# Second MLP layer of the last 12 token tiles by Strassen's algorithm, with combined weights in buffers of attention

## The chip, the core and the metric

The kernel runs on one core of a Trainium2 chip. The core has five engines that run side by side, each in its own order: TensorE (PE) multiplies matrices into PSUM, VectorE (DVE), ScalarE (ACT) and GpSimd (POOL) work element by element, and SyncE (SP) issues transfers. They meet only at semaphores. The metric is the device time of one execution in microseconds, lower is better; the median of several runs is given.

## What is computed

Cosine attention over 8 batches, 12 heads, 448 positions and head size 64, then a mixer: a low-rank mix over positions and a two-layer MLP of 768 to 3072 to 768.

```python
q_n, k_n = q / norm(q), k / norm(k)
attn = softmax(q_n @ k_n.T / tau) @ v          # (8, 12, 448, 64)
x = attn.transpose(0, 2, 1, 3).reshape(8, 448, 768)
u = x + ((x.transpose(0, 2, 1) @ U) @ V).transpose(0, 2, 1)
out = u + np.maximum(u @ w_ch1, 0.0) @ w_ch2   # (8, 448, 768), float32
```

## The kernel before

Two batches of 448 tokens make seven token tiles of 128, so there are 28 tiles in four pairs of batches. The MLP works in units: a batch of even number takes three tiles, one of odd number four. In the first layer of a unit (`up`, L942) a block of 128 hidden features is made for all tokens of the unit at once: six matmuls of 384 or 512 columns accumulate in one PSUM bank, and ScalarE or VectorE moves it through relu (L965, L967) into the one `relu` buffer, which holds 24 such blocks. In the second layer (L978) each tile's two halves of 384 output columns are 24 matmuls each, whose stationary operand is a 128 x 128 block of relu and whose moving operand is a row block of `w2_t`. VectorE adds u (L989), and SP stores the result in rows (L1003). All matmul operands are bf16, the sums and the output are float32.

Before its MLP a unit needs u, with tokens in the partitions, and its transpose `uT`, with features in the partitions. From the third batch on SP makes it by transposing DMAs (L900) into the one `uT` buffer.

Attention of later batches runs between the MLP matmuls: scores (L686) in bursts of three slots, exponentials on ScalarE (L704), products with v (L731), a reciprocal and a multiplication on VectorE (L760, L762), the low-rank projection (L815) and u (L865, L879). Queries and keys are squared, summed and scaled on VectorE and ScalarE before (L549, L553, L557, L625). Loads are issued by GpSimd's queue (L501, L524, L529), and they end some 200 us before the end.

Nothing is timed at run time. The program writes down every operation with an estimated duration, its dependences, the buffers that it takes and gives back (`Slot`, `Ring`) and a priority; `Plan.run` lays them out engine by engine, and the instructions are issued in that order. The order of streams on TensorE is fixed in a list, with the MLP's stream last, so that attention goes first where it is ready. Score bursts of batch b + 2 are tied to points of the MLP of batch b by the table `SPOTS`.

```python
work = [(i, t, c0, c0 + CH) for i, t in enumerate(tiles) for c0 in (0, CH)]
if b == B - 1:
    i, t, c0, c1 = work.pop()
    mid = c1 - 96
    work += [(i, t, c0, mid), (i, t, mid, c1)]
```

The last half tile of all is thus split into 288 and 96 columns, so that the last addition and its stores are small.

Names that the change touches: `ld_t`, `xn_t` (loaded and scaled queries and keys), `r_sq` (squares), `v_t` (v of two batches), `r_uT`, `r_relu`, `r_O` (three output tiles), `stage0` (projection and u), `mlp`, and the list of units at the end of the program.

Of the kernel before, what the change touches and what calls it, by code (L numbers as in the profile page):

```python
# [11 lines left out]
FP = mybir.dt.float32  # L12
BF = mybir.dt.bfloat16
# [256 lines left out]
def kernel(  # L270
# [42 lines left out]
    def fixed(n, shape, dt, name):  # L313

        tiles = [const.tile(shape, dt, name=f"{name}{i}") for i in range(n)]
        return tiles

    def ring(n, shape, dt, name, space=None):
        p = space or pool
        return Ring(n, lambda i: p.tile(shape, dt, name=name, tag=name, bufs=n))  # L320

    def fixed_ring(tiles):
        return Ring(len(tiles), lambda i: tiles[i % len(tiles)])

    ld_t = fixed(3, [SCH, 2, G, SC * D], BF, "qk_nat")
    xn_t = fixed(3, [SCH, 2 * SC, 128], BF, "xn")
# [5 lines left out]
    r_sq = ring(3, [SCH, G // 2, SC * D], BF, "sq")  # L332
# [8 lines left out]
    r_uT = ring(1, [128, CC, 512], BF, "uT")  # L341

    w2_t = const.tile([128, NC, C], BF, name="w2_sb")
    r_relu = Ring(1, lambda i: pool.tile([128, 4 * R + S + 4 * SC * D], FP, name="raw_uv", tag="relu", bufs=1)
                  if i == 0 else pool.tile([128, NC, 512], BF, name="relu", tag="relu", bufs=1))
# [17 lines left out]
    r_O = ring(3, [128, CH], FP, "O_sb")  # L363
# [129 lines left out]
    got, last_exp = {}, {}  # L493
# [278 lines left out]
    prev, first_v = {}, {}  # L772
# [3 lines left out]
    def columns(X, A, uT, muls, cc, a):  # L776

        c0 = 128 * cc
        mm = Slot(r_z, 1)
        st = pe_z[cc]  # L780
        X.uses += 1
        X.left += 1
        A.uses += 1
        A.left += 1
        for t in range(3):
            plan.add(Op("PE", 0.055, lambda t=t: nc.tensor.matmul(  # L786
                out=mm.tile[:, 128 * t:128 * (t + 1)], lhsT=X.tile[:, t, c0:c0 + 128], rhs=ident,
                start=(t == 0), stop=False, skip_group_check=True),
                deps=muls[2 * cc:2 * cc + 2] + [id_set] if t == 0 else (), acq=[mm, uT] if t == 0 else [],
                rel=[X] if t == 2 else []), st)  # L790
        o = plan.add(Op("PE", pe_t(384), lambda: nc.tensor.matmul(
            out=mm.tile[:, 0:384], lhsT=A.tile[:, c0:c0 + 128], rhs=V_sb[:, PAD:PAD + 384],
            start=False, stop=True, skip_group_check=True), deps=[a], rel=[A]), st)
        cs = []
        mm.uses = mm.left = 1 if cc < CC - 1 else 2
        for n in range(mm.uses):
            e, r = ("ACT/DVE", slice(0, 384)) if cc < CC - 1 else (("ACT", "DVE")[n], slice(192 * n, 192 * n + 192))
            c = plan.add(Op(e, any_t(384 // mm.uses), None, deps=[o], rel=[mm], prio=0 if cc < CC - 1 else -1))
            c.fn = lambda c=c, r=r: copy_op(c, uT.tile[:, cc, r], mm.tile[:, r])
            cs.append(c)  # L800
        return cs

    def stage0(b, X, muls):
# [6 lines left out]
        uT = Slot(r_uT, NC * CC)  # L810
# [77 lines left out]
        if by_pe:  # L888
            for ccs in ((0, 1), (2, 3), (4,), (5,)):
                z = max(0, ccs[0] - 3)  # L890
                ins = [(lambda u=u, cc=cc: u.tile[:, cc * 128:(cc + 1) * 128])
                       for cc in ccs for u in us]
# [4 lines left out]
                               [adds[z, i] for i in range(len(tiles))], [uT], list(us)))  # L897
        else:
            for i, u in enumerate(us):
                ut.append(plan.add(Op("SP", 0.1, lambda i=i, u=u: nc.sync.dma_start_transpose(  # L900
                    out=uT.tile[:, :, i * 128:(i + 1) * 128], in_=u.tile),
                    deps=[adds[0, i], adds[1, i]], acq=[uT], rel=[u], prio=0,
                    lat=("x", 0.05 * 48, 2.0))))
# [17 lines left out]
    def mlp(b, us, uT, ut):  # L921
        par = b % 2
        tiles = range(3) if par == 0 else range(3, 7)
# [3 lines left out]
        if b == B - 1:  # L927
            i, t, c0, c1 = work.pop()
            mid = c1 - 96
            work += [(i, t, c0, mid), (i, t, mid, c1)]  # L930
            us[i].uses += 1
            us[i].left += 1
# [7 lines left out]
        def up(f, mm, ccs):  # L940
            for cc in ccs:
# [5 lines left out]
                    acq=[mm] if cc == 0 else [], rel=[uT]), pe_mlp)  # L947
# [24 lines left out]
        for group in groups:  # L972
# [12 lines left out]
            for (i, t, c0, c1), mm in zip(group, mms):  # L985
# [6 lines left out]
                for bb in (b - par, b - par + 1):  # L992
                    o0 = (bb % 2) * S
                    lo, hi = max(128 * t, o0), min(128 * (t + 1), o0 + S)
                    if lo >= hi:
                        continue
                    for nn, j, p0, p1 in segments(lo - o0, hi - o0):
                        r0 = nn + o0 - 128 * t
                        by = "ACT" if 96 < w < CH and p1 - p0 < SCH else "SP"
                        O.uses += 1  # L1000
                        O.left += 1
                        plan.add(Op(by, 0.1, lambda bb=bb, j=j, p0=p0, p1=p1, r0=r0, O=O, c0=c0, c1=c1, by=by:
                            (nc.scalar if by == "ACT" else nc.sync).dma_start(  # L1003
                                out=rows(out[bb], j, p0, p1)[:, c0:c1],
                                in_=O.tile[r0:r0 + p1 - p0, 0:c1 - c0]),
                            deps=[o], rel=[O], prio=2, lat=("x", (p1 - p0) * w * 4 / 200e3, 2.0)))

        todo = bursts.get(b + 2, ()) if b else ()
# [151 lines left out]
    for b in range(B):  # L1160
        mlp(b, *state[b])
# [46 lines left out]
```

## Time and profile before

| what | value |
| --- | --- |
| runs | 578.81, 580.06 and 578.80 us, median 578.81 |
| profiled execution, first to last instruction | 576.6 us |
| TensorE clock granted, mean | 0.999 |
| L978, second layer, 128 x 384 | x1320, mean 326 ns |
| L942, first layer, 128 x 512 | x557, mean 379 ns |
| L942, first layer, 128 x 384 | x576, mean 326 ns |
| L965, relu on ACT, 128 x 512 | x84, mean 597 ns |
| L989, output addition on DVE, 128 x 384 | x55, mean 555 ns |
| L900, transposes of u by SP | x21, 3.2 us to landing |
| L1003, stores of 144 and 48 KB by SP | 2.2 and 1.8 us to landing |
| L1003, last stores, 42 and 6 KB by SP | 1.6 and 1.5 us to landing |

How to read it: a line stands for one place in the program, with the shape of its output, how often it ran and the mean duration. Matmuls overlap in TensorE's pipeline, so the mean of one is longer than the distance from one to the next. Some matmul records are missing (557 of 576). A row of slices divides the span into 40 equal parts and gives the busy share in tenths. The profiled execution is one; its span leaves out what lies before the first and after the last instruction, so it is 2.2 us below the median of the runs.

### The profile page before, as it was taken

The numbers are of one execution on the slowest core, as the hardware profiler recorded it, in microseconds if no ns is written. First come the engines' busy times: TensorE is split into PE (matmuls) and PEld (weight loads), VectorE is DVE, ScalarE is ACT, GpSimd is POOL, SyncE is SP. The second block draws the span as 40 slices with busy tenths as digits, with TensorE's granted clock in tenths as the row PEclk, the third lists the DMA queues.
The fourth block names the chain that finished last, engine by engine and source line by source line (L and its number), as shares of the span: only waits on it lengthen the run. The fifth ranks groups of instructions, "written<-read, shape, count | busy, mean of one in ns | idle before, by whom it ended". The sixth has DMA issues, their size and how long they took to land.

```text
span 576.6 us, 11689 instructions
## 1 busy us (share of the span) xinstructions
PE 567.7 (98%) x4851; PEld 326.9 (57%) x4871; DVE 286.7 (50%) x683; ACT 286.9 (50%) x475; POOL 100.3 (17%) x144
## 2 busy tenths in 40 slices
PE   8999999999999999999999999999999999999997
PEld 6565556444655665555456655564456666654565
DVE  7989969985775877386226820253012340100011
ACT  7967655577516763584645445534445344024300
POOL 8526141240050122005000400000000000000000
PEclk9999999999999999999999999999999999999999
DMA  9999998895597839567457924440040100310021
GB/s 156 205 206 141 210 194 126 126 127 78 100 101 138 108 35 144 107 109 52 57 89 119 113 14 69 95 72 2 0 69 28 43 14 15 83 41 1 2 54 56
DMA packets 132821, 50.46 MB, mean 88 GB/s; under 512 B 97920, under 2 KB 132768, under 8 KB 132768
## 3 DMA queue, kind: packets, MB, share of 16 engines
q0 software_dynamic: 72352, 25.73, 39.4%
q1 hardware_dynamic: 60384, 23.97, 20.9%
q8 instruction: 38, 0.62, 0.5%
q14 instruction: 15, 0.12, 0.1%
q10 hardware_dynamic: 32, 0.02, 0.0%
HBM read 52.02 MB, written 11.01 MB: 109 GB/s over the span
## 4 chain that ended last, share of the span: by engine, by line
PE 94%; DVE 3%; ACT 1%; issue 1%; DMA 0%; DVEq 0%
PE bank L978 39%; PE bank L942 38%; PE bank L731 8%; PE bank L686 6%; PE bank L865 2%; DVE xn L625 1%; DVE ss L557 1%; ACT attn L699 1%; PE bank L815 1%; PE bank L479 1%; DMA raw_uv<-in_q_dram 0%; DVE X_sb L762 0%; ACT sq L549 0%; DVE qkT L1019 0%; PE bank L786 0%
## 5 line engine op out<-in xcount | busy, mean ns | idle before, releaser
L978 PE MATMUL bank<-w_sb,relu 128*128 128x384 bf16 (+2 forms) x1368 | 233.4, 323 | 0.0
L942 PE MATMUL bank<-uT,w_sb 128*128 128x384 bf16 (+1 forms) x1133 | 228.3, 352 | 1.3 <-issue 0.5
L704 ACT ACTIVATE attn<-bank 128x896 bf16<-128x896 f32 (+1 forms) x163 | 139.0, 917 | 88.6 <-PE bank L686 88.4
L978 PEld LDWEIGHTS <-relu 128*128 128x128 bf16 x1368 | 127.1, 98 | 90.7 <-issue 13.6
L942 PEld LDWEIGHTS <-w_sb 128*128 128x128 bf16 x1152 | 109.4, 98 | 103.2 <-issue 7.0
L965 ACT ACTIVATE relu<-bank 128x512 bf16<-128x512 f32 (+1 forms) x159 | 86.8, 547 | 122.6 <-PE bank L942 122.2
L989 DVE TENSOR_TENSOR O_sb<-bank,u_nat 128x384 f32<-128x384 f32 (+2 forms) x57 | 31.2, 548 | 204.0 <-PE bank L978 178.8
L557 DVE TENSOR_REDUCE ss<-sq 112x8 f32<-112x512 bf16 x96 | 62.2, 673 | 6.9 <-ACT sq L549 6.4
L731 PEld LDWEIGHTS <-attn 128*128 128x128 bf16 (+1 forms) x1536 | 54.7, 97 | 10.9 <-issue 3.5
L625 DVE TENSOR_TENSOR xn<-qk_nat,inv 112x512 bf16<-112x512 bf16 x93 | 60.6, 681 | 0.1
L731 PE MATMUL bank<-v_nat,attn 128*128 128x65 bf16 (+1 forms) x1536 | 57.5, 193 | 0.9 <-DVE X_sb L762 0.4
L686 PE MATMUL bank<-qkT 64*128 64x448 bf16 (+1 forms) x384 | 46.9, 355 | 1.2 <-ACT qkT L1017 0.5
L501 POOL DMA_DIRECT2D qk_nat<-in_q_dram x24 | 17.5, 727 | 149.4 <-ACT attn L704 37.2
L524 POOL DMA_DIRECT2D v_nat<-in_v_dram x42 | 31.1, 745 | 67.7 <-PE bank L731 52.4
L762 DVE TENSOR_TENSOR X_sb<-bank,rd 128x256 bf16<-128x256 f32 x96 | 39.1, 417 | 1.6 <-DVE rd L760 0.2
L549 ACT ACTIVATE sq<-qk_nat 112x512 bf16<-112x512 bf16 x55 | 32.3, 630 | 8.3 <-DVE ss L557 8.3
L760 DVE RECIPROCAL rd<-bank 128x4 f32<-128x4 f32 x96 | 16.7, 177 | 30.3 <-PE bank L731 29.7
L879 DVE TENSOR_TENSOR u_nat<-bank,X_sb 128x384 bf16<-128x384 f32 (+2 forms) x45 | 22.0, 527 | 9.7 <-PE bank L865 9.3
L686 PEld LDWEIGHTS <-qkT 64*128 64x128 bf16 (+1 forms) x384 | 13.0, 96 | 23.5 <-issue 17.7
L967 DVE TENSOR_SCALAR relu<-bank 128x384 bf16<-128x384 f32 (+1 forms) x33 | 19.8, 601 | 11.6 <-PE bank L942 11.1
L529 POOL DMA_DIRECT2D v_nat<-in_v_dram x28 | 17.4, 626 | 8.8 <-DMA w_sb<-in_moe_w_ch_dram 5.0
L501 POOL DMA_DIRECT2D qk_nat<-in_k_dram x24 | 16.8, 702 | 3.7 <-DMA w_sb<-in_moe_w_ch_dram 3.7
(64 smaller groups left out, 189.0 us busy)
## 6 DMA issues: line engine op xcount, KB each, us to landing
qk_nat<-in_q_dram POOLq DMA_DIRECT2D x23, 224.0 KB, 4.8
qk_nat<-in_k_dram POOLq DMA_DIRECT2D x23, 224.0 KB, 5.8
w_sb<-in_moe_w_ch_dram POOLq DMA_DIRECT2D x4, 1152.0 KB, 17.7
w_sb<-in_moe_w_ch_dram POOLq DMA_DIRECT2D x8, 576.0 KB, 16.5
out_dram<-O_sb SPq DMA_DIRECT2D x15, 168.0 KB, 2.5
out_dram<-O_sb SPq DMA_DIRECT2D x16, 144.0 KB, 2.2
out_dram<-O_sb SPq DMA_DIRECT2D x16, 120.0 KB, 2.0
v_nat<-in_v_dram POOLq DMA_DIRECT2D x11, 168.0 KB, 7.5
```

The costliest lines, as they stand in the source:

```text
L501: ops = [load(lambda i=i, src=src: nc.gpsimd.dma_start(out=ld.tile[:, i, lo:lo + h1 - h0, :], in_=src[b, h0:h1].rearrange("h (s c) d -> s ...
L549: nc.scalar.activation(out=y, in_=x, func=AF.Square)
L557: lambda i=i, a0=a0, a1=a1, sq=sq: nc.vector.reduce_sum(ss.tile[:, i, a0:a1, :].rearrange("p h c -> p (h c)"), sq.tile[:, 0:a1 - a0, :].re ...
L625: nc.vector.tensor_mul(dst, src, sc)
L686: nc.tensor.matmul(out=out, lhsT=qkT.tile.rearrange("p b s -> p (b s)")[r, n0:n0 + w], rhs=qkT.tile[r, SC:2 * SC, :].rearrange("p c s -> p ...
L704: exps.append(plan.add(Op("ACT", act_t(2 * S, 0.08), lambda sc=sc, c=c, attn=attn: nc.scalar.activation(out=attn.tile[:, :, off:off + S] i ...
L731: nc.tensor.matmul(out=av.tile[:, t, 0:D + 1], lhsT=tail.tile[:, hh, 128 * t:128 * (t + 1)] if tail and j == SC - 1 else (attn if j < SC - ...
L762: muls.append(plan.add(Op("DVE", dve_t(256), lambda av=av, rd=rd, h=h: nc.vector.tensor_mul(X.tile[:, :, h * D:(h + 1) * D], av.tile[:, :, ...
L942: o = plan.add(Op("PE", pe_t(n), lambda cc=cc: nc.tensor.matmul(out=mm.tile[:, 0:n], lhsT=w1_sb[:, cc, f * 128:(f + 1) * 128], rhs=uT.tile ...
L965: nc.scalar.activation(out=relu.tile[:, f, 0:n], in_=mm.tile[:, 0:n], func=AF.Relu)
L978: nc.tensor.matmul(out=mm.tile[:, 0:c1 - c0], lhsT=relu.tile[:, f, i * 128:(i + 1) * 128], rhs=w2_t[:, f, c0:c1], start=(f == 0), stop=(f ...
L989: nc.vector.tensor_add(out=O.tile[:, 0:w], in0=mm.tile[:, 0:w], in1=us[i].tile[:, c0:c1]),
```

## The change

The first 16 tiles keep the plain second layer, in units of 3, 4, 3, 3 and 3 tiles (`UNITS`; units now cross the borders of batches). The last 12 tiles are done in six pairs. For a pair, relu is seen as 2 x 2 blocks: two tiles of tokens by even and odd blocks of hidden features; `w2_t` as even and odd row blocks by two column halves. In Winograd's form of Strassen's algorithm the product of 2 x 2 blocks takes seven block products, each of 12 matmuls with 384 columns, in place of eight.

- The first layer of a pair has 256 columns for each matmul; two hidden blocks, even and odd, share one bank and one relu of 512.
- Sums of relu blocks (S1, S2, S4, and one that overwrites a block that is no longer needed) are made on VectorE, 16 additions of 128 x 384 a pair.
- Combinations of weight blocks are made once on VectorE, 16 subtractions of 128 x 1152: T1 and T2 go into the space of the loaded and scaled queries and keys (now one tensor, `qk_t`), T4 into that of v and of the squares, and one overwrites a quarter of `w2_t`, after the last plain unit.
- Products share banks where their sums allow it. p1 is copied out by ScalarE, GpSimd adds u to it three times, and VectorE adds the banks of the other products to the results, partly while the bank goes on accumulating the next one.
- Intermediate results use seven output tiles: the three of before, and four in the unused ends of `uT` and `relu`. Those and several other buffers become fixed tensors.
- The score bursts of the last batch are tied to points of the first two pairs. The split of the last half tile goes; the store code moves to `store`.

In the counts of instructions, TensorE has 768 + 504 second-layer matmuls of 384 columns where it had 1320 and 24 each of 288 and 96; in the first layer 576 of 384, 144 of 512 and 864 of 256, where it had 576 of 384 and 576 of 512. GpSimd has 18 additions where it had none, ScalarE six more copies.

```diff
-    ld_t = fixed(3, [SCH, 2, G, SC * D], BF, "qk_nat")
-    xn_t = fixed(3, [SCH, 2 * SC, 128], BF, "xn")
+    qk_t = const.tile([128, 3 * QC + 3 * 2 * SC * 128], BF, name="qk_all")
+    ld_t = [qk_t[0:SCH, QC * i:QC * (i + 1)].rearrange("p (i h x) -> p i h x", i=2, h=G) for i in range(3)]
...
+    spare = [uT_t[:, CC * 256:].bitcast(FP), relu_t[:, 84 * 128:].bitcast(FP)]
+    r_O2 = fixed_ring([x[:, CH * i:CH * (i + 1)] for x in spare for i in range(2)] + O_t)
...
+    def seven_weights(after, qk_free, v_free):
...
+        for j0 in range(0, HF, 3):
+            x = slice(j0, j0 + 3)
+            a = minus(T1[:, x], B_[:, x, 0, 1], B_[:, x, 0, 0], qk_free)
+            c = minus(T2[:, x], B_[:, x, 1, 1], T1[:, x], [a])
+            d = minus(t4(j0), B_[:, x, 1, 0], T2[:, x], [c, *v_free])
+            e = minus(B_[:, x, 0, 1], B_[:, x, 1, 1], B_[:, x, 0, 1], [a, *after])
...
+    def mlp_seven(tiles, right, made_by):
...
+        for j in range(HF):
+            mm = Slot(r_up, 1)
+            for e in range(2):
+                for cc in range(CC):
+                    o = plan.add(Op("PE", pe_t(256), lambda j=j, e=e, cc=cc, mm=mm: nc.tensor.matmul(
+                        out=mm.tile[:, 256 * e:256 * e + 256], lhsT=w1_sb[:, cc, (2 * j + e) * 128:(2 * j + e + 1) * 128],
+                        rhs=uT.tile[:, cc, :], start=(cc == 0), stop=(cc == CC - 1)),
...
+                a = sums(lambda x=x: nc.vector.tensor_add(S1[:, x], Q[:, x, 1], Q[:, x, 3]),
+                         [ready[i][1] for i in range(j - 2, j + 1)])
+                c = sums(lambda x=x: nc.vector.tensor_sub(S2[:, x], S1[:, x], Q[:, x, 0]), [a])
+                d = sums(lambda x=x: nc.vector.tensor_sub(S4[:, x], Q[:, x, 2], S2[:, x]), [c])
+                e_ = sums(lambda x=x: nc.vector.tensor_sub(Q[:, x, 1], Q[:, x, 0], Q[:, x, 1]), [a])
...
+        p1 = product(1, a, True, False)
+        cp = plan.add(Op("ACT", 0.42, lambda: nc.scalar.copy(out=s1.tile, in_=a.tile[:, 0:CH]),
+                         deps=[p1], acq=[s1], prio=-0.5))
+        y = [plan.add(Op("POOL", 1.0, lambda y_=y_, u=u, c0=c0: nc.gpsimd.tensor_add(
+            out=y_.tile, in0=s1.tile, in1=u.tile[:, c0:c0 + CH]), deps=[cp], acq=[y_], rel=[s1, u]), pool_q)
+            for y_, u, c0 in ((y12, u1, CH), (y22, u2, CH), (y21, u2, 0))]
+        p6 = product(6, b, True, False)
+        z12 = dve(bank(tile_of(y12), tile_of(y12), b), [p6, y[0]])
+        p2 = product(2, a, False, True, [cp])
+        x11 = dve(bank(tile_of(o11), lambda: u1.tile[:, 0:CH], a), [p2], [o11], [a, u1])
+        store(tiles[0], 0, CH, o11, x11)
+        p7 = product(7, b, False, False, [z12])
+        z22 = dve(bank(tile_of(y22), tile_of(y22), b), [p7, y[1]])
+        p5 = product(5, c, True, False)
+        x22 = dve(bank(tile_of(y22), tile_of(y22), c), [p5, z22])
+        store(tiles[1], CH, C, y22, x22)
+        p4 = product(4, b, False, True, [z22])
+        x21 = dve(bank(tile_of(y21), tile_of(y21), b), [p4, y[2]], (), [b])
+        store(tiles[1], 0, CH, y21, x21)
+        p3 = product(3, c, False, True, [x22])
+        x12 = dve(bank(tile_of(y12), tile_of(y12), c), [p3, z12], (), [c])
+        store(tiles[0], CH, C, y12, x12)
...
-        if b == B - 1:
-            i, t, c0, c1 = work.pop()
-            mid = c1 - 96
-            work += [(i, t, c0, mid), (i, t, mid, c1)]
...
-    for b in range(B):
-        mlp(b, *state[b])
+    UNITS = [[(0, 0), (0, 1), (0, 2)], [(0, 3), (0, 4), (0, 5), (0, 6)], [(1, 0), (1, 1), (1, 2)],
+             [(1, 3), (1, 4), (1, 5)], [(1, 6), (2, 0), (2, 1)]]
+    for b, tiles in enumerate(UNITS):
+        mlp(b, tiles, *(state[b] if b < PE_BATCHES else columns_of(tiles)))
+    rest = [(z, t) for z in range(2, 4) for t in range(7)][2:]
...
+    for n in range(0, len(rest), 2):
+        hosts.append(mlp_seven(rest[n:n + 2], *seven))
+    (t0, l0), (t1, l1) = hosts[:2]
+    for o, at in zip(bursts[B - 1], (t0[2], t0[7], l0[0], l0[3], t1[2], t1[7], l1[0])):
+        o.deps.append(at)
```

## The prediction

> **What bounds the kernel now.** I read the page's busy shares and slices, then the chain that ended last, then the groups with shapes kept apart, and last the timeline of the stretch that the change rewrites.
>
> ```profile
> PE 567.7 (98%) x4851; PEld 326.9 (57%) x4871; DVE 286.7 (50%) x683; ACT 286.9 (50%) x475; POOL 100.3 (17%) x144
> ...
> PE   8999999999999999999999999999999999999997
> ...
> DVE  7989969985775877386226820253012340100011
> ...
> PEclk9999999999999999999999999999999999999999
> ...
> PE 94%; DVE 3%; ACT 1%; issue 1%; DMA 0%; DVEq 0%
> ```
>
> TensorE is busy in every slice at full clock, and is 94% of the chain. A busy row alone proves little, because pipelined matmuls overlap in it; the proof is the rhythm of what follows each block. VectorE, which the change loads, is at 0 to 3 tenths after slice 25 but at 4 to 8 before.
>
> ```profile
> L978 PE MATMUL bank<-w_sb,relu 128*128 128x384 bf16 x1320 | 229.5, 326 | 0.0
> L942 PE MATMUL bank<-uT,w_sb 128*128 128x512 bf16 x557 | 127.1, 379 | 1.3 <-issue 0.5
> L731 PEld LDWEIGHTS <-attn 128*128 128x128 bf16 x1344 | 47.5, 97 | 7.4
> L553 DVE TENSOR_TENSOR sq<-qk_nat 112x512 bf16<-112x512 bf16 x35 | 13.8, 417 | 7.3 <-DMA qk_nat<-in_q_dram 7.2
> L625 DVE TENSOR_TENSOR xn<-qk_nat,inv 112x512 bf16<-112x512 bf16 x93 | 60.6, 681 | 0.1
> L551 POOL TENSOR_TENSOR sq<-qk_nat 112x512 bf16<-112x512 bf16 x4 | 4.2, 1054 | 1.3 <-DVE ss L557 1.1
> ```
>
> ```profile
> 368.58 1.14 PE L731 MATMUL bank<-v_nat,attn 128*128 128x65 bf16 x32
> 369.56 1.95 PE L978 MATMUL bank<-w_sb,relu 128*128 128x384 bf16 x11
> ```
>
> ```profile
> 513.55 0.60 ACT L965 ACTIVATE relu<-bank 128x512 bf16<-128x512 f32 x1 [0.65 <-PE bank L942]
> 514.85 0.60 ACT L965 ACTIVATE relu<-bank 128x512 bf16<-128x512 f32 x1 [0.70 <-PE bank L942]
> ...
> 561.54 0.56 DVE L989 TENSOR_TENSOR O_sb<-bank,u_nat 128x384 f32<-128x384 f32 x1 [3.34 <-PE bank L978]
> 565.44 0.56 DVE L989 TENSOR_TENSOR O_sb<-bank,u_nat 128x384 f32<-128x384 f32 x1 [3.34 <-PE bank L978]
> 569.34 0.56 DVE L989 TENSOR_TENSOR O_sb<-bank,u_nat 128x384 f32<-128x384 f32 x1 [3.34 <-PE bank L978]
> 572.28 0.46 DVE L989 TENSOR_TENSOR O_sb<-bank,u_nat 128x288 f32<-128x288 f32 x1 [2.38 <-PE bank L978]
> 573.30 0.26 DVE L989 TENSOR_TENSOR O_sb<-bank,u_nat 128x96 f32<-128x96 f32 x1 [0.56 <-PE bank L978]
> ```
>
> The group means (326 and 379 ns) are latencies. The pace is in the timeline: a relu follows every six 512-column matmuls, 1.295 us apart, so 216 ns each; an output add follows every 24 matmuls of 384 columns, 3.90 us apart, so 162.5 ns each; the 288- and 96-column pieces took 2.94 and 1.02 us for 24, so 122.5 and 42.5 ns. All four are columns/2.4 ns plus 2.5 ns. From 40 us to the end, starts one after another at that pace leave gaps of some 8 us in all, about 2 us of them after 320 us. The end is therefore set by the number of matmul columns.
>
> **What the Trainium skill says.** "TensorE: Matmul & The Clock Gate", section "Wait — 56ns, not 53.3ns?", gives N/2.4 + about 2.5 ns for a warm stream: the trace agrees at four widths. Its section "Back-to-back issue gap" puts a stream with weight loads at about 81 ns for N=128 and 131 ns for N=512; the trace shows 216 ns at 512, so that line doesn't hold here, but it feeds a rival. "VectorE: DVE Perf Modes", "The perf-mode tier table", says that tensor_tensor reaches two elements a cycle in bf16 from SBUF: the squares (417 ns for 512, against 681 ns for the multiply with a broadcast scale) agree. "SBUF — State Buffer", "SBUF: two separate sides", says a VectorE instruction with two SBUF inputs and a GpSimd one that reads SBUF exclude each other for a whole instruction; no row of before tests this.
>
> **The change, part by part.** Counts are from the instruction order of the two programs. The streams of TensorE agree up to about 325 us (the end of the third unit); so do the loads. What follows is therefore all in the second half.
>
> 1. Second layer of 12 token tiles. Removed: 552 matmuls of 384 columns and 24 pairs of 288 + 96: 552 x 0.1625 + 24 x (0.1225 + 0.0425) = 93.7 us. Added: 6 pairs x 7 products x 12 = 504 x 0.1625 = 81.9 us. Together -11.8 us.
>
> 2. First layer. Before: 576 matmuls of 384 and 576 of 512 columns. After: 576 of 384, 144 of 512, 864 of 256. The columns are equal; there are 432 more fixed parts. A 256-column matmul isn't in the trace; between 96 and 512 the pace is linear, so 109.2 ns: 864 x 0.1092 - 432 x 0.216 = +1.1 us. Bounds: +0 (no fixed part) to +19 (rival C). The weight load of 98 ns beside each doesn't show: 32 attention products of 65 columns, each with a full load of its own, take 0.98 us from 368.58 to 369.56, 31 ns each.
>
> 3. Weight combinations, once: 16 VectorE subtractions of 128 x 1152 bf16. From the squares: 417 ns = 512 at two per cycle (267) + 150, so 600 + 150 = 750 ns, of which some 85 overlap the next one (two squares took 0.75 us together at 38.07): 0.667 us each, 10.7 us. They stand in VectorE's queue among the first pair's work. I lay the two queues side by side from the last attention product of batch 6 to the tenth matmul of p6, which needs the last T2 part. TensorE: 116 up matmuls x 0.1092 = 12.7, 6 x 0.1625 = 1.0 for u, 0.5 for the rank projection, three score bursts 0.70 + 0.67 + 0.67 = 2.0 (12 small ones at 121.88, 6 wide ones at 366.11 took this), 21 x 0.1625 = 3.4: 19.6 us. VectorE: 14 combinations x 0.667 = 9.3, 16 sums of relu blocks x 0.27 = 4.3 (384 elements: 200 + 150 - 85 ns), 6 u adds x 0.49 = 2.9, a copy 0.5, two relus x 0.62 = 1.2, and 0.8 until it starts: 19.0 us, plus its own waits for relus and u. VectorE is thus about full, and its waits (the last sums need the last relu, 0.9 us after the first layer's end) make T2 some 0.5 us late; a GpSimd addition that holds the shared port adds up to 0.9. I take +0.8 us; bounds 0 (waits overlap) and +3 (both relus late too, which holds up the first layer's banks). The T4 part and the overwritten B12 are wanted a product or more later.
>
> 4. Per pair, 16 sums (5 us of VectorE in 29.4 us) run while the first layer runs; only the last four come after it, and p6 wants them 3.4 us after its end while they are done by about 2.4. Covered by p1; without it, about 2 us a pair.
>
> 5. Chain between products. p1's bank is copied by ScalarE (0.48 us), three GpSimd additions start from it, VectorE adds the banks (0.56 us each). GpSimd for 384 elements: 1054 ns for 512, so about 0.8 to 1.0. p7 waits for z12, which waits for the first GpSimd addition: 0.7 + 1.0 + 0.1 + 0.6 = 2.4 us after p1's end, and p7 starts 3.9 us after it (p6, p2 between). The others have more room. Behind p7's wait stand all later TensorE work, so this cover matters: it fails when a GpSimd addition exceeds 2.4 us. Price taken 0, bounds 0 and rival B. GpSimd has no loads left by then.
>
> 6. Buffers. Next pair's columns are transposed by SP at the end of the first layer: two issues of 1.24 us, landing in 3.2 (longest 6.9) us, wanted 13.7 us later (84 x 0.1625). SP's stores of the pair before stand ahead of them and are landed. The two banks that the first layer alternates between are refilled each 1.31 us, and a relu takes 0.60 plus some 0.2: no wait, as with 512 columns. Unit changes (11 instead of 8) and 42 product heads with waits already met: +0.4 us, bounds 0 and 1.5; the last layer of before shows no loss at such heads.
>
> 7. Tail. The last add is 384 wide, not 96: 0.56 against 0.26, +0.3. Its stores are 48 and 144 KB, not 6 and 42: landing 2.2 instead of 1.6, +0.6. Together +0.9 us.
>
> Sum: -11.8 + 1.1 + 0.8 + 0.4 + 0.9 = -8.6 us. Against the profiled execution (span 576.6): 568.0. The median of the runs, 578.81, lies 2.2 us above the span; so 570.2 us.
>
> **Rivals.** A: VectorE is the bound in the first pair. If the subtractions run at one element a cycle (strided reads of the weight rows), each is 1.35 us instead of 0.75, 14 of them +8.4 us in a queue without slack, and relu sums add some 2: about 579, no change. If it is only the two-port exclusion and bunched waits, +3: 573. For: VectorE is full there. Against: the squares' rate. Chance of the mild form 0.13, of the full form 0.03.
>
> B: GpSimd's addition is long. Place: p7 of each pair, six times. At d us each the loss is 6 x (d - 2.4); equal to the gain from d = 3.8. The 1.05 us at 512 elements speaks against it; float data and mixed types are what it doesn't show. Chance 0.02 (at 5 us: 586).
>
> C, ending slower: 256 columns don't cover a weight load in a stream. Place: the 864 first-layer matmuls. If the 25 ns that the skill's 81 ns lies above 56 also come on top here, 134 ns, +21 us: 591. It decides from 119 ns a matmul (8.6 us / 864 = 10 ns more). Against: 31 ns a matmul with its load in attention. Chance 0.04.
>
> **How the numbers follow.** Forecast as summed 0.78, mild A 0.13: both faster. Full A 0.03: within 0.3%, which is 1.7 us and about what a measurement of this kernel can tell from no change. B and C 0.06: slower. Floor of the range: no stalls at all, -11.8 + 1.1 + 0.9 = -9.8, 569.0, and 0.4 for the projection's own error: 568.6. Ceiling: mild A plus the upper price of the heads, 574.2. Outside it lies about 0.15: full A, B, C and the end of mild A.
>
> **What would show it.** Right: relus of a pair 1.31 us apart in the first layer (12 of them); output adds 1.95 us apart between products; a pair 15.7 + 13.7 = 29.4 us from first relu to first relu. The first pair alone shows TensorE waiting for VectorE, under 1.5 us. Wrong: a relu rhythm above 1.4 us (C), p7 starting with a wait for VectorE behind GpSimd in each pair (B), subtractions above 1 us (A).

## The result, and the profile after

The changed kernel took 570.35 us (median of four runs, 569.83 to 571.55) against 579.13 us for the kernel before beside it (four runs, 578.80 to 580.06): ratio 0.9852, 95% interval 0.9836 to 0.9867. The forecast was 570.2. The profiled execution took 571.55 us, its span is 569.0 us, 7.6 us shorter than the span before. Three executions with far longer times are left out of all medians and ratios below: 971 and 1492 us of the layout with the squares' order, whose only trace is of the former, and 832 us of the kernel before beside it.

Where that came from is read in two parts. Up to 244.8 us, where the fourth unit begins (with 512 columns before, with 384 now), the two programs issue TensorE's work in the same order, so the same instruction can be compared in both traces: there the changed kernel is **2.2 us late** from 33 us on. From there to the end it gains 7.6 + 2.2 = **9.8 us**, which is what the counted matmuls and the tail give (-11.8 + 1.1 + 0.9 = -9.8) with no stall at all; TensorE's list of waits is empty from 40 us to the end. So the total was met by two errors that nearly cancel: 1.2 us of stalls in the second part that did not come, and a loss at the start that the prediction did not have.

Page of the changed kernel, busy shares, slices and chain:

```profile
PE 559.8 (98%) x5207; PEld 362.1 (64%) x5207; DVE 337.8 (59%) x815; ACT 284.5 (50%) x472; POOL 118.1 (21%) x162
...
DVE  7889969987674786477437722479444532323232
...
PEclk9899999999999999999999999999999999999999
...
PE 94%; DVE 3%; DMA 1%; ACT 1%; issue 0%; POOL 0%; DVEq 0%; ACTq 0%; POOLq 0%
```

TensorE is still 94% of the chain. VectorE, at 0 to 5 tenths in the last 15 slices before, now has 2 to 9 there; the 9 is the 28th slice (384 to 398 us), in the first pair, with the weight combinations. The clock row has an 8 in its second slice: a new thing, to which the experiments come back.

Timeline of ScalarE in the fifth pair's first layer, changed kernel (start, us, engine, line, operation, idle before and its releaser):

```profile
508.71 0.60 ACT L1017 ACTIVATE relu<-bank 128x512 bf16<-128x512 f32 x1 [0.71 <-PE bank L1007]
510.04 0.60 ACT L1017 ACTIVATE relu<-bank 128x512 bf16<-128x512 f32 x1 [0.72 <-PE bank L1007]
511.35 0.60 ACT L1017 ACTIVATE relu<-bank 128x512 bf16<-128x512 f32 x1 [0.71 <-PE bank L1007]
512.66 0.60 ACT L1017 ACTIVATE relu<-bank 128x512 bf16<-128x512 f32 x1 [0.71 <-PE bank L1007]
```

A relu each 1.31 us stands for twelve 256-column matmuls: 109 ns each. The last four pairs, which have no attention between them, begin 29.4 to 29.5 us apart (446.94, 476.48, 505.85, 535.22 us).

Timeline of the first pair of the changed kernel, around the point where TensorE needs the last part of T2:

```profile
394.10 1.63 PE L1042 MATMUL bank<-qk_all,relu 128*128 128x384 bf16 x9
...
394.58 0.35 DVE L1033 TENSOR_TENSOR relu<-relu 128x384 bf16<-128x384 bf16 x1
394.85 0.35 DVE L1032 TENSOR_TENSOR relu<-relu 128x384 bf16<-128x384 bf16 x1
395.12 0.75 DVE L976 TENSOR_TENSOR qk_all<-w_sb,qk_all 128x1152 bf16<-128x1152 bf16 x1
395.14 2.84 POOL L1064 TENSOR_TENSOR uT<-uT,u_nat 128x384 f32<-128x384 f32 x1 [68.18 <-ACT uT L1062]
...
395.66 0.74 PE L695 MATMUL bank<-qkT 64*128 64x448 bf16 x6
395.79 0.75 DVE L976 TENSOR_TENSOR w_sb<-w_sb 128x1152 bf16<-128x1152 bf16 x1
...
396.33 0.66 PE L1042 MATMUL bank<-qk_all,relu 128*128 128x384 bf16 x3
396.46 0.75 DVE L976 TENSOR_TENSOR sq_all<-w_sb,qk_all 128x1152 bf16<-128x1152 bf16 x1
```

VectorE's last part of T2 (out `qk_all`, from `w_sb` and `qk_all`) ends at 395.87 (395.12 + 0.75); the tenth matmul of p6 starts at 396.33, in its turn after a burst of six score matmuls (L695). VectorE is busy for 18.49 of the 18.7 us before 395.9, so it is as full as it was laid out, but T2 is 0.46 us early, not 0.5 late.

### The profile page after: what moved, and what is told of

It is laid out like the page before. It is cut to its first block, busy times and chain, and to the rows that moved or that the text cites. A ratio compares the mean times of both kernels' runs of the same rounds, so it can differ in the third digit from the quotient of the medians.

```text
span 569.0 us, 12604 instructions
## 1 busy us (share of the span) xinstructions
PE 559.8 (98%) x5207; PEld 362.1 (64%) x5207; DVE 337.8 (59%) x815; ACT 284.5 (50%) x472; POOL 118.1 (21%) x162
## 4 chain that ended last, share of the span: by engine, by line
PE 94%; DVE 3%; DMA 1%; ACT 1%; issue 0%; POOL 0%; DVEq 0%; ACTq 0%; POOLq 0%
PE bank L1134 22%; PE bank L1098 22%; PE bank L1007 17%; PE bank L1042 14%; PE bank L740 8%; PE bank L695 6%; PE bank L895 2%; DMA qk_all<-in_k_dram 1%; PE bank L488 1%; DVE qk_all L634 1%; ACT attn L708 1%; PE bank L845 1%; DVE X_sb L771 0%; DVE ss L566 0%; DVE ln L586 0%
## 5 line engine op out<-in xcount | busy, mean ns | idle before, releaser
L1134 PE MATMUL bank<-w_sb,relu 128*128 128x384 bf16 x768 | 136.3, 326 | 0.0
L1098 PE MATMUL bank<-uT,w_sb 128*128 128x384 bf16 (+1 forms) x720 | 135.3, 337 | 0.0
L1134 PEld LDWEIGHTS <-relu 128*128 128x128 bf16 x768 | 71.0, 98 | 53.4 <-issue 10.7
L1098 PEld LDWEIGHTS <-w_sb 128*128 128x128 bf16 x720 | 67.3, 98 | 54.4 <-issue 6.7
L1007 PE MATMUL bank<-uT,w_sb 128*128 128x256 bf16 x864 | 97.6, 273 | 0.0
L1007 PEld LDWEIGHTS <-w_sb 128*128 128x128 bf16 x864 | 83.8, 98 | 12.4 <-issue 1.8
L1017 ACT ACTIVATE relu<-bank 128x512 bf16<-128x512 f32 x68 | 40.6, 597 | 100.5 <-PE bank L1007 100.5
L1121 ACT ACTIVATE relu<-bank 128x384 bf16<-128x384 f32 (+1 forms) x84 | 42.7, 509 | 48.2 <-PE bank L1098 47.7
L566 DVE TENSOR_REDUCE ss<-sq_all 112x8 f32<-112x512 bf16 x96 | 61.9, 672 | 5.4 <-ACT sq_all L558 5.0
L634 DVE TENSOR_TENSOR qk_all<-qk_all,inv 112x512 bf16<-112x512 bf16 x93 | 60.7, 680 | 0.1
L1042 PE MATMUL bank<-w_sb,relu 128*128 128x384 bf16 x288 | 50.4, 326 | 0.0
L1145 DVE TENSOR_TENSOR O_sb<-bank,u_nat 128x384 f32<-128x384 f32 x32 | 17.7, 555 | 51.9 <-PE bank L1134 47.6
L695 PE MATMUL bank<-qkT 64*128 64x448 bf16 (+1 forms) x384 | 47.3, 357 | 1.1 <-ACT qkT L1160 0.5
L558 ACT ACTIVATE sq_all<-qk_all 112x512 bf16<-112x512 bf16 x53 | 31.1, 629 | 7.6 <-DVE ss L566 7.6
```

Source lines behind the costliest of these rows:

```text
L566: lambda i=i, a0=a0, a1=a1, sq=sq: nc.vector.reduce_sum(ss.tile[:, i, a0:a1, :].rearrange("p h c -> p (h c)"), sq.tile[:, 0:a1 - a0, :].re ...
L634: nc.vector.tensor_mul(dst, src, sc)
L695: nc.tensor.matmul(out=out, lhsT=qkT.tile.rearrange("p b s -> p (b s)")[r, n0:n0 + w], rhs=qkT.tile[r, SC:2 * SC, :].rearrange("p c s -> p ...
L1007: o = plan.add(Op("PE", pe_t(256), lambda j=j, e=e, cc=cc, mm=mm: nc.tensor.matmul(out=mm.tile[:, 256 * e:256 * e + 256], lhsT=w1_sb[:, cc ...
L1017: nc.scalar.activation(out=dst, in_=mm.tile[:, 0:512], func=AF.Relu)
L1042: o = plan.add(Op("PE", pe_t(CH), lambda j=j: nc.tensor.matmul(out=mm.tile[:, 0:CH], lhsT=left[k](j), rhs=right[k](j), start=(first and j ...
```

## The experiments

**Theories.** P: the gain is that of the matmul columns, seven products for eight. L: the layout of the buffers alone costs about 1 us at the start. S, formed after the first runs: that cost is one buffer of GpSimd's squares. Rivals: the start differs only because loads land a little differently from run to run; VectorE (A) or GpSimd (B) are near a limit in each pair, and the forecast was right by luck. "By the ratios" below means the difference of two ratios times the 578.6 us of the kernel before; each ratio has an interval of 0.4 to 0.9 us to either side.

### The layout alone

The kernel before, with the merged and fixed buffers and nothing else of the change:

```diff
-    ld_t = fixed(3, [SCH, 2, G, SC * D], BF, "qk_nat")
+    qk_t = const.tile([128, 3 * QC + 3 * 2 * SC * 128], BF, name="qk_all")
+    ld_t = [qk_t[0:SCH, QC * i:QC * (i + 1)].rearrange("p (i h x) -> p i h x", i=2, h=G) for i in range(3)]
...
-    r_sq = ring(3, [SCH, G // 2, SC * D], BF, "sq")
+    sq_t = const.tile([128, 3, G // 2 * SC * D], BF, name="sq_all")
+    r_sq = fixed_ring([sq_t[0:SCH, i].rearrange("p (h x) -> p h x", h=G // 2) for i in range(3)])
...
-    r_O = ring(3, [128, CH], FP, "O_sb")
+    r_O = fixed_ring(O_t)
```

> The kernel before with only the buffers of the changed one (queries, keys and their scaled forms in one tensor, squares, uT, relu and output tiles as fixed tensors); the work is the same. In the profile of the changed kernel the first 30 us are 2.2 us later than before, 0.9 us of it a key load that landed at 7.71 instead of 6.36 us, and the clock fell to 0.57 between 20 and 24 us. Theory L (the buffers' placement is the cause): 580 to 581.5 us, mean clock 0.995 to 0.997, the slow stretch in the profile again. Rival C (chance of the landing in that execution): 579.1 us within 0.5, clock 0.999.

Measured: 579.59 us (16 runs) against 578.57 (30 runs), ratio 1.0017 (1.0010 to 1.0024). The layout costs 1.0 us on its own, without any Strassen arithmetic. By the ratio that is 580.1 us on the 579.13 of the first comparison, the lower end of theory L. Its second sign did not come: the trace has the full clock (1.000) from start to end, though 11 of the 16 runs have a mean of 0.996 or 0.997.

### Eight products in the pairs

The changed kernel with its pairs, its layout and its 256-column first layer, but eight plain block products for each pair in place of seven, and no sums, combinations or GpSimd additions:

```diff
-        p1 = product(1, a, True, False)
...
+        for i, t in enumerate(tiles):
+            for h in range(2):
+                for j in range(HF):
+                    for e in range(2):
+                        o = plan.add(Op("PE", pe_t(CH), lambda i=i, h=h, j=j, e=e, mm=mm: nc.tensor.matmul(
+                            out=mm.tile[:, 0:CH], lhsT=Q[:, j, 2 * e + i], rhs=w2_t[:, 2 * j + e, h * CH:h * CH + CH],
...
```

> The changed kernel with its pairs, first layer of 256 columns and attention's places, but eight plain block products in place of seven: no combinations of weights, no sums of relu blocks, no GpSimd additions. Theory P (TensorE's matmuls alone set the time): 576 second-layer matmuls of the pairs instead of 504, 72 x 0.1625 = 11.7 us more than the changed kernel, 582.0 us, 1.005 of before. Rival D (the combinations and additions cost time on the path that goes with them): less than that, 579 to 581.

Measured: 582.32 us (five runs), ratio 1.0058 (1.0044 to 1.0071). The eighth product is 72 matmuls of 384 columns, 11.7 us at the pace of the timeline; by the ratios, 1.0058 against 0.9852, it costs 11.9 us. P stands: what the seven products need besides matmuls is hidden, as far as ratios with these intervals can tell.

### GpSimd's first addition four times

```diff
-        y = [plan.add(Op("POOL", 1.0, lambda y_=y_, u=u, c0=c0: nc.gpsimd.tensor_add(
-            out=y_.tile, in0=s1.tile, in1=u.tile[:, c0:c0 + CH]), deps=[cp], acq=[y_], rel=[s1, u]), pool_q)
+        y = [plan.add(Op("POOL", 1.0, lambda y_=y_, u=u, c0=c0: [nc.gpsimd.tensor_add(
+            out=y_.tile, in0=s1.tile, in1=u.tile[:, c0:c0 + CH]) for _ in range(4 if y_ is y12 else 1)],
...
```

> The changed kernel with the first of the three GpSimd additions of a pair done four times over (the same numbers are written again). Theory W (p7 waits for z12, which waits for this addition, and has 1.15 us of room in the fourth pair: z12 ends at 496.91, p7 starts at 498.05): 3 x 0.91 us more minus 1.15 is 1.6 us a pair, six pairs, about 9 us: 579 to 580. Rival N (p7 is not held by it, or something else gives way): 570.4 within 1 us.

Measured: 577.77 us (14 runs), ratio 0.9980 (0.9971 to 0.9989), 7.4 us above the changed kernel by the ratios. Waits of TensorE in this run (line, waited for: us in total, times, longest), and the fourth pair's timeline:

```profile
PE bank L1042 <- DVE uT L1057: 2.9, 2, 1.7
PE bank L1042 <- DVE O_sb L1057: 2.4, 2, 1.2
PE bank L1042 <- DVE relu L1057: 1.2, 1, 1.2
```

```profile
496.93 0.48 ACT L1062 COPY uT<-bank 128x384 f32<-128x384 f32 x1 [1.29 <-PE bank L1042]
497.49 4.75 POOL L1064 TENSOR_TENSOR relu<-uT,u_nat 128x384 f32<-128x384 f32 x5 [25.13 <-ACT uT L1062]
...
501.40 0.56 DVE L1057 TENSOR_TENSOR relu<-bank,relu 128x384 f32<-128x384 f32 x1 [4.44 <-POOL relu L1064]
...
502.01 1.30 PE L1042 MATMUL bank<-w_sb,relu 128*128 128x384 bf16 x7 [1.22 <-DVE relu L1057]
```

The mechanism of rival B is real: four additions of 0.91 us make z12 late, and p7 starts 1.2 us late in a pair. At one addition the same chain has room, as the timeline of the changed kernel shows: copy at 494.35, GpSimd at 494.90, z12 from 496.35 to 496.91, p7 at 498.05, so 1.1 us to spare; by these times an addition of about 2.05 us would use it up. The expectation was 1.6 us too high: the wait is 1.2 us in four pairs and 1.7 in the first, where 1.6 was expected in each of six, and the listed waits, 6.5 us, are those of five pairs; the second pair, which has attention's matmuls between its products, loses nothing.

### The weight combinations twice

```diff
-        def minus(out, a, b, deps):
-            o = plan.add(Op("DVE", 0.06 + 3 * CH * 0.00053, lambda: nc.vector.tensor_sub(out, a, b), deps=deps, prio=3))
+        def minus(out, a, b, deps, n=2):
+            o = plan.add(Op("DVE", 0.06 + 3 * CH * 0.00053, lambda: [nc.vector.tensor_sub(out, a, b) for _ in range(n)],
...
```

Twelve of the sixteen are issued twice; the four that overwrite their own operand once.

> The changed kernel with 12 of the 16 weight subtractions on VectorE done twice (those that don't overwrite their input). Theory F (VectorE is full in the first pair, with 0.46 us of room before the tenth matmul of p6, from 395.87 to 396.33 in the profile): 11 of them stand before that matmul, 11 x 0.667 = 7.3 us minus 0.46: +6.9, 577.2 us. Rival R (its waits leave room that the busy row doesn't show): 570.4 to 573. The first GpSimd addition took 2.84 us instead of 0.91 beside these subtractions: if VectorE's two-input operations shut it out, it takes longer still here; if it was the first use of that operation, 2.84 again.

Measured: 581.82 us (four runs), ratio 1.0055 (1.0041 to 1.0068), 11.7 us above the changed kernel by the ratios; the expectation had 6.9 of them. Timeline of VectorE and GpSimd in the first pair of this run, its waits, and two windows (us, then busy time of each engine, clock, DMA share, GB/s):

```profile
399.75 2.13 DVE L976 TENSOR_TENSOR qk_all<-w_sb 128x1152 bf16<-128x1152 bf16 x2
400.30 0.98 POOL L1065 TENSOR_TENSOR uT<-uT,u_nat 128x384 f32<-128x384 f32 x1 [73.87 <-ACT uT L1063]
401.24 2.40 POOL L1065 TENSOR_TENSOR relu<-uT,u_nat 128x384 f32<-128x384 f32 x2
401.81 1.06 DVE L1032 TENSOR_TENSOR relu<-relu 128x384 bf16<-128x384 bf16 x1
402.80 1.06 DVE L1034 TENSOR_TENSOR relu<-relu 128x384 bf16<-128x384 bf16 x1
...
403.78 0.34 DVE L1033 TENSOR_TENSOR relu<-relu 128x384 bf16<-128x384 bf16 x1
```

```profile
PE bank L1043 <- DVE qk_all L976: 4.0, 1, 4.0
PE bank L1008 <- DVE relu L1020: 2.4, 2, 2.3
```

```profile
393.10:396.60 3.50, 3.34 (x19) 1.72 (x16) 3.50 (x8) 0.60 (x1) 0.00 (x0) 0.51 0.00 0
...
406.70:410.20 3.50, 3.50 (x40) 2.59 (x39) 2.14 (x6) 0.00 (x0) 0.00 (x0) 0.51 0.02 5
```

TensorE waits 6.4 us for VectorE, near the 6.9 that the full queue promised. The rest is mostly not waiting. The wait of 2.3 us ends at 392.23 and that of 4.0 us at 405.64; about 1 us after each, the granted clock falls to half for some 3.5 us, which loses 1.7 us each time. With 0.9 us of further waits, at the matmuls for u (0.57 and 0.29 us, L895), the sum is 6.4 + 3.4 + 0.9 = 10.7 of the 10.9 us by which this span (579.9) exceeds the changed kernel's (569.0). The full queue of the prediction was thus real, and so was the mechanism of rival A; its price per lost microsecond was too low.

Of GpSimd's first addition neither forecast came true: it took 0.98 us. So first use is not what made it 2.84 us in the changed kernel. Here VectorE is the one that is held: two subtractions beside it took 2.13 us, where two in a row take 1.42 (0.67 + 0.75).

### Which buffer of the layout

Two runs of the kernel before with one part of the layout each: the six q/k buffers as views of one tensor, and all the others.

```diff
-    ld_t = fixed(3, [SCH, 2, G, SC * D], BF, "qk_nat")
-    xn_t = fixed(3, [SCH, 2 * SC, 128], BF, "xn")
+    qk_t = const.tile([128, 3 * QC + 3 * 2 * SC * 128], BF, name="qk_all")
```

> The kernel before with one part of the new layout alone: the six q/k buffers become views of one buffer; squares, columns, relu and output buffers stay as they were. If the 1.0 us that the whole layout costs comes from this part (the waits at its start were for q/k buffers), the time is 579.6 us, ratio 1.0017. If it comes from the fixed squares' ring or the other fixed buffers, 578.6, ratio 1.000.

> The kernel before with the other part of the new layout: the squares', columns', relu and output buffers fixed; the q/k buffers stay separate. The opposite of the run with the merged q/k buffers: 578.6 us if those cause the 1.0 us, 579.6 us if these do. If both give about 0.5, the cost is no single wait but the start's sensitivity to when buffers come free.

Measured: 578.41 us (13 runs), ratio 0.9998 (0.9990 to 1.0006), for the q/k buffers; 579.64 us (21 runs), ratio 1.0018 (1.0012 to 1.0025), for the others. Only the second part costs. What differs is seen 15 us after the start. GpSimd and VectorE, kernel before, and then the run with the other buffers fixed:

```profile
14.91 2.09 POOL L551 TENSOR_TENSOR sq<-qk_nat 112x512 bf16<-112x512 bf16 x2 [0.18 <-DVE ss L557]
```

```profile
15.93 0.17 DVE L577 TENSOR_SCALAR ln<-ln 112x32 f32<-112x32 f32 x1
16.13 0.35 DVE L579 RECIPROCAL inv<-ln 112x32 f32<-112x32 f32 x1
```

```profile
15.68 2.04 POOL L555 TENSOR_TENSOR sq_all<-qk_nat 112x512 bf16<-112x512 bf16 x2 [0.84 <-DVE ss L561]
```

```profile
16.11 0.64 DVE L581 TENSOR_SCALAR ln<-ln 112x32 f32<-112x32 f32 x1
16.79 0.35 DVE L583 RECIPROCAL inv<-ln 112x32 f32<-112x32 f32 x1
```

The second two squares of GpSimd start 0.84 us after the first two instead of 0.18. Three squares' buffers are in use; before, the third square gets the one that was freed first, and with a fixed number for each it gets the next in number, which VectorE's sum `ss` reads 0.6 us longer. So the late square begins 0.43 us ahead of VectorE's small operation on `ln`, which then takes 0.64 us instead of 0.17: it ends at 16.75, as the square does (15.68 + 1.04). Before, it fell on the change from one square to the next, at 15.95. Everything behind it is about 0.5 us later, also the scaled q/k that TensorE waits for. Its first matmul on them, kernel before, and then the run with the other buffers fixed:

```profile
17.61 0.37 PE L479 MATMUL bank<-ident,xn 112*128 112x112 bf16 x4 [0.29 <-DVE xn L625]
```

```profile
18.32 0.37 PE L483 MATMUL bank<-ident,xn 112*128 112x112 bf16 x4 [0.82 <-DVE xn L629]
```

The changed kernel shows the same three figures (0.84, 0.64 and 0.82).

### The squares' buffers in the order in which they are freed

```diff
-    r_sq = fixed_ring([sq_t[0:SCH, i].rearrange("p (h x) -> p h x", h=G // 2) for i in range(3)])
+    sq_free = [sq_t[0:SCH, i].rearrange("p (h x) -> p h x", h=G // 2) for i in range(3)]
...
+                    at.append(sq_free.pop(0))
...
+                    sq_free.append(at[0])
```

This edit was made on the kernel before with the whole layout, and on the changed kernel.

> The whole layout on the kernel before, but the three squares' buffers are handed out in the order in which they were freed, as the kernel before has it, instead of by number. Theory S: the 1.0 us of the layout comes from GpSimd's third square, which by number gets a buffer that is freed 0.66 us later and then runs beside VectorE's small operation on ln (0.64 us instead of 0.17), which delays the first scaled q/k. Then GpSimd's third square starts within 0.2 us of the end of the second, ln takes 0.17 us, and the ratio is 1.000 (578.6 us). Rival: the start is only sensitive to when loads land, and any layout with these buffers fixed shows it: 1.0017 again (579.6).

> The changed kernel with the squares' buffers handed out in the order in which they were freed. Theory S: about 1.0 us less than the changed kernel, 569.2 us, ratio 0.9835; the first scaled q/k is not late. Rival (landing of loads): 570.1, ratio 0.985.

The changed kernel as it is, once more, ran beside the two parts of the layout:

> The changed kernel itself, beside the other runs of this job: ratio to before 0.985 (570.1 us on 578.7). If the late start of the profiled execution (2.2 us by 28 us, half of it under a lower granted clock) is a trait of that one execution, this profile's span is about 568.0 and its start is late by about 1 us; if it belongs to the kernel, the span is 569 again.

Measured: the layout with this order 578.75 us (11 runs) against 578.75 (16 runs), ratio 1.0000 (0.9991 to 1.0008); the changed kernel with this order **568.70 us** (five runs, 568.52 to 569.67), ratio 0.9836 (0.9822 to 0.9850); the changed kernel itself 570.09 us (four runs, 568.96 to 571.00) against 578.49, ratio 0.9852 (0.9838 to 0.9867), span 569.2. GpSimd and VectorE in the changed kernel with this order:

```profile
13.06 4.21 POOL L564 TENSOR_TENSOR sq_all<-qk_all 112x512 bf16<-112x512 bf16 x4 [1.18 <-DVE ss L571]
```

```profile
16.15 0.17 DVE L593 TENSOR_SCALAR ln<-ln 112x32 f32<-112x32 f32 x1
```

The four squares follow one another, `ln` takes 0.17 us, and the layout costs nothing. (In the trace of the layout with this order the four squares follow one another too, 4.21 us in all; `ln` takes 0.26 us there.) S is shown on the kernel before: intervals of 1.0010 to 1.0024 without and 0.9991 to 1.0008 with the order do not touch. On the changed kernel the gain of about 1 us agrees, though those two intervals overlap.

What the late square itself costs is read from when TensorE starts the same matmul in each trace. The numbers are us later than in the kernel before:

| trace | a score matmul at 15.93 us | first matmul on the scaled q/k, at 17.61 us | a first-layer matmul at 40.20 us |
| --- | --- | --- | --- |
| changed kernel, first profile | 0.83 | 1.37 | 2.22 |
| changed kernel, second profile | 0.03 | 0.56 | 1.46 |
| layout alone | 0.74 | 1.28 | 1.14 |
| layout, other buffers only | 0.18 | 0.72 | 1.54 |
| layout, q/k buffers only | 0.22 | 0.21 | 0.65 |
| changed kernel, squares in the order freed | 0.23 | 0.27 | -0.11 |

From the first column to the second, the four traces with the squares' buffers by number lose 0.53 or 0.54 us, and the two others 0.04 at most. The first column differs between two executions of the same kernel and goes with the landing of loads: the second load of keys landed at 7.71 us in the first profile of the changed kernel, at 6.77 in the second and at 6.36 before. The third column grows by 0.4 to 0.9 us in the four traces that have a stretch of half clock at about 20 us, and shrinks in the two that have none. So of the 2.2 us of the first profile 0.8 come with the loads, 0.5 with the squares and 0.9 with the lower clock. The second profile has the span of the first (569.2) for another reason: it is 0.8 us ahead of it from 40 us to the last matmul, but its last two stores took 1.76 us to issue instead of 0.78.

The rest of the 1.0 us goes with a lower mean clock: 0.994 to 0.997 in 35 of 49 runs with the squares' buffers by number (two layout runs, three of the changed kernel and its split tail), in 6 of 33 with the order of before, and in 21 of 79 for the kernel before itself. Among runs with a mean of 0.999 and more, the layout alone costs 0.75 us (mean 579.22 us against 578.47 beside it). The late square is neither needed nor enough for a lower clock in a single execution: the trace of the q/k buffers has the stretch at half clock without it, that of the layout alone has the late square at full clock. In the changed kernel's first profile (windows as above):

```profile
20.00:24.00 4.00, 3.94 (x46) 2.63 (x44) 3.41 (x9) 2.60 (x5) 3.02 (x5) 0.57 1.16 210
24.00:40.00 16.00, 15.15 (x256) 10.38 (x254) 13.74 (x50) 14.13 (x20) 4.81 (x7) 1.00 1.25 206
```

Four us at 0.57 lose 1.7 us of clock, which is 0.003 of the span: a mean of 0.997 is one such stretch.

### The tail split again

The changed kernel with its last product in 288 + 96 columns, as the kernel before has its last half tile; then the same with the 96 columns in a bank of their own, together with the squares' order. The edit shown is that of the second run:

```diff
-        p3 = product(3, c, False, True, [x22])
+        cuts = [(0, CH, c)] if tiles[-1] != (3, 6) else [(0, CH - 96, c), (CH - 96, CH, Slot(r_mm, 1))]
...
+            early = add(CH - 96, CH, c, [p5, z12])
```

> The changed kernel with its very last product (p3 of the last pair) computed in 288 + 96 columns, each with its own add and store, as the last output block of the kernel before is. If the tail term of the sum (+0.9 us: 0.3 of the longer add, 0.6 of the longer stores) is right, this wins back 0.8 us against the changed kernel (12 extra heads of 2.5 ns cost 0.03): ratio to before about 0.9838, 569.2 us against 578.6. Rival: the end is set by the landing of stores that were issued earlier (the 144 KB of the pair's other tile), then nothing changes: ratio 0.985.

> The changed kernel with the squares' buffers in the order in which they were freed, and with the last product in 288 + 96 columns, the 96 in a bank of their own, so that they don't wait for the add of the 288 (0.5 us in the first run of the split tail); p5's part of these columns is added earlier. If the two gains add up (1.0 and 0.8): 568.4 us, ratio 0.982. If the end is set by the stores' own landing, the tail brings nothing: 569.2.

Measured: 569.70 us (four runs), ratio 0.9847 (0.9834 to 0.9861), for the first, which had the wait that its one bank forces (`PE bank L1085 <- DVE O_sb L1091: 0.5, 1, 0.5` in its waits); 568.66 us (four runs), ratio 0.9830 (0.9816 to 0.9844), for the second, against 568.70 with the squares' order alone. No gain is resolved; one of 0.8 us is not excluded by these intervals. The two profiles show what stands against it. End of the run with both edits, then of the one with the squares' order alone:

```profile
561.98 1.44 SPq L968 DMA_DIRECT2D out_dram<-uT  x2
562.80 0.77 DVE L1091 TENSOR_TENSOR O_sb<-bank,O_sb 128x288 f32<-128x288 f32 x2 [0.85 <-PE bank L1099]
563.52 1.79 SPq L968 DMA_DIRECT2D out_dram<-O_sb  x4
```

```profile
562.45 0.56 DVE L1064 TENSOR_TENSOR O_sb<-bank,O_sb 128x384 f32<-128x384 f32 x1 [1.34 <-PE bank L1049]
563.03 0.78 SPq L968 DMA_DIRECT2D out_dram<-O_sb  x2
```

Split, the last tile has four stores, which SP issues one after another in 1.79 us, after an issue before them that took until 563.42; whole, it has two in 0.78 us. In both, and in the first run with the split tail, 6.4 us pass from the first matmul of the last product (561.13, 560.30 and 561.56) to the end of the span (567.6, 566.7 and 568.0). The version with the squares' order is the fastest shown, with or without the split.

## Why the prediction was right

By its own steps, against the traces and runs:

1. **Second layer, -11.8 us: right.** The eight-product run puts the seven products at 11.9 us below eight, for 11.7 by the columns.
2. **First layer, +1.1 us: right.** 109 ns a matmul. Rival C (134 ns, 591 us) is excluded. (The step's upper bound of +19 us doesn't fit that rival's own 864 x 25 ns, which is +21 us above the step; nothing hung on it.)
3. **Weight combinations, +0.8 us: the laid-out queue was right, its end was not.** Durations were 748 ns for the predicted 750, and VectorE had 0.2 us of idle time in 18.7. But T2 was 0.46 us early where 0.5 late was forecast, and the exclusion that was to cost VectorE up to 0.9 us fell on GpSimd instead: its addition at 395.14 took 2.84 us beside three subtractions, against 0.91 alone. Measured: no wait of TensorE. The distance to a loss is small, which the doubled combinations show.
4. **Sums of relu blocks, 0: right**, at 0.35 us each.
5. **GpSimd chain, 0: right.** 0.91 us an addition, 1.1 us of room. Rival B is excluded, and its place is the right one: with four additions p7 waits. Its limit is lower than forecast, about 2.05 us an addition for 2.4.
6. **Buffers, units and heads, +0.4 us: too high; measured 0.** From 40 us to the end TensorE has no listed wait.
7. **Tail, +0.9 us: right in size.** From the start of the last matmul to the end of the span 3.57 us before (573.06 to 576.63) and 4.60 after (564.42 to 569.02), so +1.0; in the second profile of the changed kernel it is 5.6, for its slower last issue. That splitting the product wins it back was not predicted, and no run shows it.

**What failed** is the sentence ahead of the steps, that the same order on TensorE and the same loads leave the first half as it was. The order of instructions was the same, up to 244.8 us and not to 325, but not what they wait for: a fixed number for each squares' buffer in place of the first one free cost 1.0 us, a term that the sum had at nothing. It stood against the 1.2 us of steps 3 and 6, which did not come; that the total came out only 0.15 us off the median is luck. What the steps have right, the 9.8 us of columns and tail, less this 1.0 us, is 8.8, as measured (579.13 - 570.35). With that cost taken away the changed kernel is at 568.7 us, where the prediction's own floor without stalls (569.0) was.

The reading of VectorE's row was off too: it is at 0 to 5 tenths after slice 25 and at 0 to 9 before, not 0 to 3 and 4 to 8. No term rests on it.

One thing stays open: how the late square makes the lower clock more frequent. The layout without and with the squares' order had it in 11 of 16 and 2 of 11 runs, but single traces go both ways, and no run changed TensorE's waits at the start by other means.

## What to carry to other kernels

Count matmul columns first: where TensorE is the bound, eight products made seven were worth their columns, as long as the added chains are laid against the products that cover them. When a change renames or merges buffers, compare what each early instruction waits for, and not only the order of instructions: a ring that hands out by number isn't the same as one that hands out what is free. A total that fits is no proof; split it where the two programs stop being alike.

## What the hardware showed beside this

GpSimd and VectorE held each other up in both directions: GpSimd's addition took 2.84 us beside VectorE's subtractions instead of 0.91; VectorE's relu sums took 1.06 us beside GpSimd's additions instead of 0.35, and its 0.17 us operation on `ln` 0.64 us. The Trainium skill, "SBUF — State Buffer", section "SBUF: two separate sides", says that whichever starts first keeps the shared port for the whole instruction; the first two agree, and in the first GpSimd came through only after the third of the subtractions that followed one another (the last ended at 397.21, the addition at 397.98). The operation on `ln` has one input and 32 elements; it was held too, to the end of GpSimd's square. The section names such an instruction only if it runs in a two-port mode; no run shows in which mode it ran.

TensorE's waits of 2.3 and 4.0 us, in the run with doubled combinations, were each followed by some 3.5 us at half clock, so that 6.4 us of waits came with 3.4 us more. Waits of 1.2 to 1.7 us, in the run with four GpSimd additions, were not: its clock is 1.00 from 40 to 560 us.
